# FFN blocks that carry attention: the value products of two tiles in one run, fourteen buffers for exponentials

## The chip, the cores and the metric

The kernel runs on one core of a Trainium2 chip. TensorE (PE) multiplies; ScalarE (ACT), VectorE (DVE) and GpSimd (POOL) work on elements; SyncE (SP) issues nearly all DMAs. Each engine takes its own instructions in order and waits for the others at semaphores. The metric is the device time of one execution in microseconds (us), the median over runs; lower is better.

## The reference

One transformer block on 2048 rows of width 576, in fp32: `h = x + attention(layernorm(x))`, `out = h + ffn(layernorm(h))`.

- Attention has 32 query heads of width 18 and one head of keys and values that all of them share. Scores are scaled by 18^-0.5, softmaxed over all 2048 keys (no mask), multiplied with the values, and projected by `wo` (576 x 576).
- The FFN is a bilinear gate without a nonlinearity: `((x @ w_gate) * (x @ w_up)) @ w_down`, inner width 4608.

## The kernel before

The 2048 rows are four blocks of 512. Keys, values and queries come first, together with the attention of block 0. From then on the FFN of block b is run with the attention of later blocks in between, so that ACT's exponentials lie beside TensorE's FFN products. The last FFN (block 3) has no attention beside it and is written another way (`last_block`). The schedule is the program's own order: the text of the functions sets the order of each engine's instructions, and buffers are rings, so an instruction that takes a buffer waits until the last reader of the old content is done.

**One FFN tile** (`ffn`, loop over `f`, 36 per block) makes 128 of the 4608 inner columns for 512 rows. It has 27 steps `j` (9 slices of the width, each as high*high, high*low and low*high of numbers split into two fp32r parts, called hi and lo). A step is two matmuls at once: the gate product `pg` on rows 0 to 63 of the array and the up product `pu` on rows 64 to 127. While attention is left (`on`), `pg` and `pu` come from a ring of three PSUM banks (`ps_r`), which the down product uses too; later they are two halves of one `gu` tile. At the end of a tile ACT copies `pg` out of PSUM (`g`, line 1063), and DVE multiplies it with `pu` into `hf` (line 1067).

**Two tiles make a pair.** After an odd tile (`k` = 1) the two `hf` are turned into operands `A` (tile `room`): sums `S` on DVE (lines 937 to 940), then splits into hi and lo (`left_first`, `left`, `left_sums`; `split` at lines 96 and 97 casts, and DVE subtracts). At the end of the next even tile the down product of that pair runs (`down`): 42 matmuls, each on the full 128 x 128 array, in 14 stages of three. Every stage's result is added to the residual `h`, by DVE straight from PSUM (line 994), or by an ACT copy into one of the `tmp` buffers (line 998) and a POOL add (line 999). For the last pair of a block the product is a plain one (line 958).

**Attention in between** is counted in pairs of heads: `pair` does two score matmuls of 56 rows side by side (line 701) into one of two score tiles in PSUM (`ps_s`, two banks each), and ACT takes the exponentials of the 128 x 1024 scores into a buffer `P` (line 702). Every two pairs complete one key tile `t`, and `flush` then multiplies the exponentials waiting in `pend` with the values: four matmuls per key tile that each use 32 of the array's columns (line 706); on the chip each of them is two passes, so the trace has 4096 of them for 2048 in the program. Before the change a tile with attention has pairs at `j` = 0, 4, ..., 24 and one after step 26, eight in all, and ends with a flush of four key tiles (32 recorded passes, 8 groups of four).

So TensorE works in three shapes: two halves of 64 rows (FFN and scores), the full array (down, projections `yo` at line 832, transposes at line 888), and four strips of 32 columns (values). The order before is: odd tile, values, even tile, values, down product, and again.

**Weights.** `load_w` loads the gate and up weights of a tile (576 KB) into `wr` (two buffers), `split_w` splits them into `ws` (POOL cast, DVE subtraction); it is called at `j` = 3 for the next tile and starts the load for the tile after it. `load_wd` loads the down weights, seven pieces per pair, into ten `wdo` buffers. `weight_sums` makes sums of weights for the last block with POOL during the first two FFNs.

At the end of a block `spread` transposes the next block's normalised rows (`xh`) into `X`.

Of the kernel before, what the change touches and what calls it, by code (L numbers as in the profile page):

```python
# [57 lines left out]
class Block:  # L58
# [744 lines left out]
    def load_wo_0(self):  # L803

        self.wo_0 = self.wp.tile([P, 2, 5, D], F32R, tag="X", bufs=1, name="wo_0")
        rs = [self.wp.tile([P, 2, D], F32, tag="wr", bufs=2, name=f"wo_r{i}") for i in range(2)]
# [9 lines left out]
    def project(self, b, c):  # L816
# [4 lines left out]
        for s in range(NQ):  # L821
            sl = slice(s * P, (s + 1) * P)
            for n in range(2):
# [9 lines left out]
                if b and c == 4 and (s, n) in ((0, 1), (2, 0)):  # L833
                    z = self.tmp[:, self.n_tmp % 5]
                    self.n_tmp += 1
                    self.act.copy(z, y[:, :HD])
# [28 lines left out]
    def normal(self, b):  # L865
# [3 lines left out]
        for s in range(NQ):  # L869
            xh = self.p_tile([P, 640], f"xh2_{b}_{s}") if b else self.wp.tile([P, 640], F32, tag="wdo", bufs=WD_BUFS, name=f"xh2_0_{s}")  # L870
# [34 lines left out]
    def load_w(self, n):  # L905

        if n < NF * (NB - 1):
            r = self.wr[n] = self.wp.tile([P, 9, P], F32, tag="wr", bufs=2, name=f"wr{n}")
            self.sp.dma_start(r, self.wgu[n % NF])

    def split_w(self, n):
        if n < NF * (NB - 1):
# [3 lines left out]
            self.load_w(n + 2)  # L916
# [9 lines left out]
    def left_first(self, n, hf):  # L926

        m = 2 if plain(n) else 1
        self.split(self.A[:, 0, 0:m], self.A[:, 1, 0:m], hf[:, 0:m * HT].rearrange("p (a q) -> p a q", a=m))

    def left(self, n, hf):
# [9 lines left out]
        self.split(A[:, 0, m:m + 2], A[:, 1, m:m + 2], hf[1].rearrange("p (a q) -> p a q", a=2))  # L941

    def left_sums(self):
        self.split(self.A[:, 0, 3:7], self.A[:, 1, 3:7], self.S)

    def down(self, b, pair):
# [4 lines left out]
        if pair == NC - 1:  # L951
# [8 lines left out]
            def add(s, n):  # L960
                hs, y = h[:, s, n * HD:(n + 1) * HD], ys.pop((s, n))[:, :HD]
                if n:
                    z = self.tmp[:, self.n_tmp % 5]
# [20 lines left out]
        for i, (t, bank, (x, w), first, (s, n), on_dve) in enumerate(STAGES):  # L984
# [10 lines left out]
            else:  # L995
                z = self.tmp[:, self.n_tmp % 5]
# [5 lines left out]
    def room(self):  # L1002
# [5 lines left out]
        self.tmp = self.hh.tile([P, 5, HD], F32, tag="tmp", bufs=1, name="tmp")  # L1008
        self.n_tmp = 0

    def ffn(self, b):
# [6 lines left out]
        for f in range(NF):  # L1018
# [12 lines left out]
            for c in range(9):  # L1031
                for wk, xk in ((0, 0), (0, 1), (1, 0)):
                    if on and not last and j % 4 == 0 and self.more(b + 2):
# [15 lines left out]
                    if j == 21 and b == f == 0:  # L1049
                        self.flush(len(self.pend))  # L1050
# [11 lines left out]
            g = self.hh.tile([P, TB], F32, tag="g", bufs=1, name=f"g{n_}")  # L1062
            act.copy(g, pg)  # L1063
# [11 lines left out]
            self.flush(len(self.pend))  # L1075
# [6 lines left out]
        if end:  # L1082
            del X, pg, pu, gu, w, ps, hf, g, self.X
# [8 lines left out]
    def ahead(self):  # L1092
# [58 lines left out]
        for i in range(-LEAD, 0):  # L1151
            if i == 4 - LEAD:
                yield
                sets = [self.wp.tile([P, 4 * HT], F32R, tag="wr", bufs=2, name=f"wrs{i}") for i in range(2)]
# [50 lines left out]
    def down_pairs(self, b, pairs):  # L1205
# [4 lines left out]
        for i, (bank, (x, w), first, (s, n)) in enumerate(QUAD):  # L1210
            W = [self.wdo.pop((b, p, w)) for p in pairs]
            for t in range(2):
# [9 lines left out]
                else:  # L1222
                    z = self.tmp[:, self.n_tmp % 5]
# [8 lines left out]
    def last_block(self, ahead, D):  # L1232
# [45 lines left out]
        for p in range(NC):  # L1278
# [73 lines left out]
            g = self.hh.tile([P, TB], F32, tag="g", bufs=1, name=f"gl{p}")  # L1352
# [125 lines left out]
    def run(self):  # L1478
# [16 lines left out]
        with ExitStack() as st:  # L1495
# [8 lines left out]
            self.G = cp.tile([P, 64], F32R, name="G")  # L1504
            self.mx = cp.tile([H, 8], F32, name="mx")
            st.enter_context(tc.manual_schedule())
            with tc.tile_pool(name="p0q", bufs=1) as self.p0q:
                self.wq_in, self.wq = self.wq, {}
                self.XT = [self.p0q.tile([P, 9, TB], F32R, tag=f"XT{b}", name=f"XT{b}") for b in range(NB)]
                with tc.tile_pool(name="qb", bufs=2) as self.qb:  # L1510
# [24 lines left out]
            self.wp, self.hh, self.p2 = pool("w", 2), pool("hid", 4), pool("P2", 1)  # L1535
# [19 lines left out]
            self.load_w(1)  # L1555
# [12 lines left out]
            self.split_w(0)  # L1568
            self.cast = self.act.copy
# [14 lines left out]
P_BUFS = 6  # L1584

# [4 lines left out]
WD_BUFS = 10  # L1590
# [145 lines left out]
```

## Time and profile before

| | before |
|---|---|
| median of 3 runs | 2279.18 us (2277.54 to 2280.16) |
| span of the profiled execution | 2277.7 us |
| TensorE matmul busy | 2251.0 us, 99% of the span |
| ACT / DVE / POOL busy | 66% / 56% / 32% |
| exponentials (line 702) | 1024, 1027 ns each |
| value passes (line 706) | 4096 |
| down products (line 988) | 2142 matmuls, 51 runs of 42 |

The span runs from the first to the last instruction of the profiled execution; it is the time of that execution that the page gives, 1.5 us under the median of the timed runs. Matmuls are pipelined and their ends are modelled, so "busy" does not say how fast TensorE works: the distance from one start to the next does. PE is the matmul, PEld the loading of its weights. In a row of groups the numbers after the bar are busy time and the mean duration of one instruction in ns, then idle time before them. In a row of the timeline stand the start in us, the duration in us, the engine, the line, and the count of instructions that follow each other; a bracket shows idle time before, and what ended it.

### The profile page before, as it was taken

What the parts mean: (1) busy time and instruction counts of PE and PEld (TensorE: products, weight loads), DVE (VectorE), ACT (ScalarE), POOL (GpSimd) and SP (SyncE); (2) the same over time, 40 slices, a digit from 0 to 9 for tenths busy, and PEclk for the clock granted to TensorE, in tenths of its full rate; (3) what the DMA queues carried; (4) which work ended last, traced back from release to release, by engine and by line L of the source; (5) the groups of instructions that cost most, each with busy time, mean ns of one, the idle gap of its engine ahead of it and who ended that gap; (6) DMA issues with size and microseconds to landing.
All of it is one profiled execution on the core that took longest, in us unless ns stands there. A gap on an engine that the chain in (4) does not pass through costs nothing.

```text
span 2277.7 us, 46397 instructions
## 1 busy us (share of the span) xinstructions
PE 2251.0 (99%) x17972; PEld 1640.2 (72%) x17972; DVE 1267.0 (56%) x2184; ACT 1512.4 (66%) x2061; POOL 719.5 (32%) x820
## 2 busy tenths in 40 slices
PE   7999999999999999999999999999999999999999
PEld 5333345777677777777777777777777788999999
DVE  8555645444445446454545455544434477778776
ACT  7888876767676766667666766667676724555553
POOL 4445401333233333323333332322222244222222
PEclk9999999999999999999999999999999999999999
DMA  5879843545455554645555544654343345677775
GB/s 175 266 247 300 287 162 99 168 157 158 158 172 166 164 180 149 206 140 168 165 164 171 167 160 146 204 175 145 113 126 109 105 160 174 207 247 237 233 248 172
DMA packets 200438, 407.05 MB, mean 179 GB/s; under 512 B 22638, under 2 KB 54510, under 8 KB 200214
## 3 DMA queue, kind: packets, MB, share of 16 engines
q1 hardware_dynamic: 197621, 393.42, 54.0%
q0 software_dynamic: 2592, 10.62, 1.5%
q8 instruction: 143, 2.34, 0.4%
q14 instruction: 82, 0.66, 0.1%
HBM read 317.27 MB, written 74.55 MB: 172 GB/s over the span
## 4 chain that ended last, share of the span: by engine, by line
PE 83%; DVE 2%; ACT 1%; issue 0%; DMA 0%; SPq 0%; POOL 0%; ACTq 0%; DVEq 0%
PE pg L1036 23%; PE acc L706 15%; PE y L988 13%; PE s L701 9%; PE gs L1252 8%; PE yq L1217 4%; PE pu L1036 3%; PE yo L832 3%; PE gu L1036 2%; PE gs L1259 2%; PE y L958 1%; ACT P L702 1%; PE tx L888 0%; DVE room L97 0%; DVE ws L97 0%
## 5 line engine op out<-in xcount | busy, mean ns | idle before, releaser
L702 ACT ACTIVATE P<-s 128x1024 f32<-128x1024 f32 x1024 | 1025.6, 1027 | 273.7 <-PE s L701 195.3
L1036 PE MATMUL pu<-X,ws 64*128 64x512 f32 x2565 | 694.3, 390 | 0.0
L1036 PE MATMUL pg<-X,ws 64*128 64x512 f32 x2565 | 693.5, 389 | 0.1
L1036 PEld LDWEIGHTS pg<-X,ws 64*128 64x128 f32 x2565 | 476.2, 186 | 72.5 <-DMA wsum<-in_wgs_dram 0.8
L706 PE MATMUL acc<-P,V 128*32 128x512 f32 x4096 | 491.0, 599 | 0.7 <-ACT P L702 0.6
L1036 PEld LDWEIGHTS pu<-X,ws 64*128 64x128 f32 x2565 | 473.8, 186 | 4.9 <-ACT tmp L965 0.3
L701 PE MATMUL s<-q,kT 56*128 56x512 f32 x2048 | 441.5, 422 | 4.6 <-ACT P L702 3.5
L999 POOL TENSOR_TENSOR h<-h,tmp 128x288 f32<-128x288 f32 x306 | 238.4, 807 | 598.2 <-ACT tmp L998 597.1
L701 PEld LDWEIGHTS s<-q,kT 56*128 56x128 f32 x2048 | 199.7, 184 | 203.3 <-ACT P L702 118.8
L988 PEld LDWEIGHTS y<-wdo,room 128*128 128x128 f32 x2142 | 289.6, 188 | 43.2 <-issue 34.8
L988 PE MATMUL y<-wdo,room 128*128 128x288 f32 x2142 | 303.6, 300 | 1.3 <-DVE h L994 1.3
L706 PEld LDWEIGHTS acc<-P,V 128*32 128x32 f32 x4096 | 114.8, 109 | 246.9 <-issue 234.4
L994 DVE TENSOR_TENSOR h<-h,y 128x288 f32<-128x288 f32 x408 | 176.1, 453 | 199.8 <-PE y L988 199.6
L998 ACT COPY tmp<-y 128x288 f32<-128x288 f32 x306 | 122.1, 399 | 240.8 <-PE y L988 222.3
L1067 DVE TENSOR_TENSOR hf<-pu,g 128x512 f32<-128x512 f32 x95 | 65.7, 692 | 303.1 <-ACT g L1063 303.1
L96 POOL CAST ws<-wr 128x1152 fp32r<-128x1152 f32 x108 | 127.1, 1177 | 315.0 <-PE pu L1036 238.2
L97 DVE TENSOR_TENSOR ws<-wr,ws 128x1152 fp32r<-128x1152 f32 x108 | 184.6, 1709 | 64.0 <-POOL ws L96 59.7
L1200 POOL TENSOR_TENSOR wsum<-wsum,wsum 128x512 f32<-128x512 f32 x72 | 99.7, 1385 | 137.6 <-DMA wsum<-in_wgs_dram 137.4
L97 DVE TENSOR_TENSOR room<-S,room 128x1024 fp32r<-128x1024 f32 x51 | 62.5, 1226 | 132.8 <-ACT room L96 132.8
L1217 PE MATMUL yq<-wdo,XW 128*128 128x288 f32 x504 | 86.1, 297 | 0.1
L1036 PE MATMUL gu<-X,ws 64*128 64x512 f32 x702 | 82.0, 390 | 0.0
L839 DVE TENSOR_TENSOR h<-h,yo 128x288 f32<-128x288 f32 x154 | 63.4, 452 | 30.1 <-PE yo L832 26.8
(262 smaller groups left out, 2633.3 us busy)
## 6 DMA issues: line engine op xcount, KB each, us to landing
wdo<-wd_dram SPq DMA_DIRECT2D x492, 288.0 KB
wr<-in_wgu_dram SPq DMA_DIRECT2D x108, 576.0 KB
wsum<-in_wgs_dram SPq DMA_DIRECT2D x108, 256.0 KB
wd_dram<-wd_room SPq DMA_DIRECT2D x20, 1008.0 KB
wsum_dram<-wsum SPq DMA_DIRECT2D x72, 256.0 KB
raw<-wsum_dram SPq DMA_DIRECT2D x72, 256.0 KB
q<-q_dram SPq DMA_DIRECT2D x64, 216.0 KB
raw<-in_wgs_dram SPq DMA_DIRECT2D x54, 256.0 KB
```

The source lines that it names most:

```text
L96: (copy or self.cast)(hi, src)
L97: self.dve.tensor_tensor(lo, src, f32(hi), ALU.subtract)
L701: self.pe.matmul(s_[:, i], self.kT[o:o + 56, t * P:(t + 1) * P], q[o:o + 56, pr], start=True, stop=True)
L702: self.act.activation(p_, s_, AF.Exp, scale=SCALE)
L706: self.pe.matmul(acc[32 * j:32 * j + 32, :], self.V[:, t, :], Ps[j // 2][:, j % 2, :], start=(t == 0), stop=(t == NT - 1), skip_group_chec ...
L988: pe.matmul(y[:, :HD], m[:, t * P:(t + 1) * P], k, start=(first and j == 0), stop=(j == 2), skip_group_check=True)
L994: dve.tensor_tensor(hs, hs, y[:, :HD], ALU.add)
L998: act.copy(z, y[:, :HD])
L999: pool.tensor_tensor(hs, hs, z, ALU.add)
L1036: pe.matmul(ps, w[o:o + 64, wk, c], X[o:o + 64, xk, c], start=(j == 0), stop=(j == 26))
L1217: pe.matmul(y[:, :HD], A[:, k, x, t * P:(t + 1) * P], v[:, l], start=(first and z == j == 0), stop=(z == len(pairs) - 1 and j == 2), skip_ ...
L1252: pe.matmul(bank[:, g * HT:(g + 1) * HT], W[:, wk, c, g], X[:, 2 * xk + c], start=(first and g == c == wk == xk == 0), stop=(c == 1 and wk ...
```

## The change

- In a tile with attention, an odd tile no longer flushes (`if not k or last`). The value products of two tiles (eight key tiles) run together at the end of the even tile, in front of the down product.
- The pairs stand at other steps: in an even tile at `j` = 0, 4, ..., 20 and two after step 26, in an odd tile as before (0, 4, ..., 24 and one after step 26). The last tile of a block, which had none, gets eight pairs at every third step, and a flush.
- The ring of buffers for exponentials grows from 7 to 14 (`P2_BUFS` = 8 beside the 6 of `P_BUFS`).
- Room for it: one `wr` buffer instead of two (the load of tile n + 2 is now issued at `j` = 14, or 9 without attention, after the split of tile n + 1); nine `wdo` instead of ten; three `tmp` instead of five; no `g`, ACT copies `pg` into `hf`, and DVE multiplies in place; `G` in a pool that is given back; 2048 bytes of scratch for DMA descriptors per partition.
- The casts of `left_first`, `left` and `left_sums` move from ACT to POOL (line 96).

TensorE at the end of an odd tile. Here `s` are scores, `pg` and `pu` the FFN products, `acc` the values; the first three rows are steps of the odd tile, the last ones of the even tile that follows. Before:

```order
L1036 MATMUL pg_15526<-X_10340,ws_15333 128x512
L1036 MATMUL pu_15527<-X_10340,ws_15333 128x512
L701 MATMUL s_0_3_1_15649<-q_0_14923,kT 128x512 x2
L706 MATMUL acc_0_15662<-P_0_0_0_15529,V 32x512 x2
L706 MATMUL acc_0_15662<-P_0_0_1_15547,V 32x512 x2
L706 MATMUL acc_0_15662<-P_0_1_0_15562,V 32x512 x2
L706 MATMUL acc_0_15662<-P_0_1_1_15576,V 32x512 x2
L706 MATMUL acc_0_15662<-P_0_2_0_15604,V 32x512 x2
L706 MATMUL acc_0_15662<-P_0_2_1_15618,V 32x512 x2
L706 MATMUL acc_0_15662<-P_0_3_0_15636,V 32x512 x2
L706 MATMUL acc_0_15662<-P_0_3_1_15650,V 32x512 x2
L701 MATMUL s_0_4_0_15683<-q_0_14923,kT 128x512 x2
```

and in the change:

```order
L1035 MATMUL pg_15493<-X_10336,ws_15285 128x512
L1035 MATMUL pu_15494<-X_10336,ws_15285 128x512
L701 MATMUL s_0_3_1_15616<-q_0_14894,kT 128x512 x2
L701 MATMUL s_0_4_0_15632<-q_0_14894,kT 128x512 x2
L1035 MATMUL pg_15630<-X_10336,ws_15508 128x512
L1035 MATMUL pu_15631<-X_10336,ws_15508 128x512
```

The values are gone from this place; the last scores of the odd tile, the first scores of the even tile and its first `pg` and `pu` follow each other. Over the whole program the array's shape changes 567 times before and 471 times in the change. The joined run of two tiles stands in the program 44 times.

ACT at the same place, before:

```order
L702 ACTIVATE P_0_3_0_15636<-s_0_3_0_15635 128x1024
L1063 COPY g_15647<-pg_15526 128x512
L702 ACTIVATE P_0_3_1_15650<-s_0_3_1_15649 128x1024
L96 CAST room<-hf_15654 128x512
L96 CAST room<-ob_10593 128x512
L702 ACTIVATE P_0_4_0_15684<-s_0_4_0_15683 128x1024
L702 ACTIVATE P_0_4_1_15702<-s_0_4_1_15701 128x1024
L702 ACTIVATE P_0_5_0_15715<-s_0_5_0_15714 128x1024
L96 CAST room<-S 128x1024
L702 ACTIVATE P_0_5_1_15731<-s_0_5_1_15730 128x1024
```

and in the change:

```order
L702 ACTIVATE P_0_3_0_15603<-s_0_3_0_15602 128x1024
L1062 COPY hf_15614<-pg_15493 128x512
L702 ACTIVATE P_0_3_1_15617<-s_0_3_1_15616 128x1024
L96 CAST room<-ob_10586 128x512
L702 ACTIVATE P_0_4_0_15633<-s_0_4_0_15632 128x1024
L702 ACTIVATE P_0_4_1_15649<-s_0_4_1_15648 128x1024
L702 ACTIVATE P_0_5_0_15662<-s_0_5_0_15661 128x1024
L702 ACTIVATE P_0_5_1_15678<-s_0_5_1_15677 128x1024
```

The casts of `hf` and `S` have left ACT's queue; the order of exponentials and of the copy of `pg` among each other is the same.

POOL in FFN tiles without attention (block 2, near its end), one row after another. Before, its queue holds the casts of two tiles' weights and the six adds of a down product, here for two pairs:

```order
L96 CAST ws_26397<-wr_26007 128x1152
L96 CAST ws_26526<-wr_26155 128x1152
L999 TENSOR_TENSOR h_16896<-h_16896,tmp 128x288 x6
L96 CAST ws_26730<-wr_26400 128x1152
L96 CAST ws_26868<-wr_26529 128x1152
L999 TENSOR_TENSOR h_16896<-h_16896,tmp 128x288 x6
```

and in the change, for one pair:

```order
L96 CAST ws_28344<-wr_28217 128x1152
L96 CAST room<-hf_28332 128x256
L96 CAST room<-hf_28406 128x512
L96 CAST room<-S 128x1024
L96 CAST ws_28426<-wr_28363 128x1152
L998 TENSOR_TENSOR h_16912<-h_16912,tmp 128x288 x6
```

Three casts of the operands now stand in front of the second weight cast and of the adds.

The diff, cut to its core:

```diff
-        i = self.p_next = (self.p_next + 1) % (P_BUFS + (self.p2 is not None))
+        i = self.p_next = (self.p_next + 1) % (P_BUFS + (P2_BUFS if self.p2 is not None else 0))
...
     def load_w(self, n):
...
-            r = self.wr[n] = self.wp.tile([P, 9, P], F32, tag="wr", bufs=2, name=f"wr{n}")
+            r = self.wr[n] = self.wp.tile([P, 9, P], F32, tag="wr", bufs=1, name=f"wr{n}")
...
             self.split(w[:, 0], w[:, 1], r, self.nc.gpsimd.tensor_copy)
-            self.load_w(n + 2)
...
     def left_first(self, n, hf):
...
-        self.split(self.A[:, 0, 0:m], ..., a=m))
+        self.split(self.A[:, 0, 0:m], ..., a=m), self.nc.gpsimd.tensor_copy)
...
     def left_sums(self):
-        self.split(self.A[:, 0, 3:7], self.A[:, 1, 3:7], self.S)
+        self.split(self.A[:, 0, 3:7], self.A[:, 1, 3:7], self.S, self.nc.gpsimd.tensor_copy)
...
-                    z = self.tmp[:, self.n_tmp % 5]
+                    z = self.tmp[:, self.n_tmp % NTMP]
...
     def ffn(self, b):
...
-                    if on and not last and j % 4 == 0 and self.more(b + 2):
+                    if on and j in (PAIRS[2] if last else PAIRS[k]) and self.more(b + 2):
                         self.pair()
...
                     if j == 3:
                         self.split_w(n_ + 1)
+                    if j == (14 if on else 9):
+                        self.load_w(n_ + 2)
...
-                    if j == 21 and b == f == 0:
-                        self.flush(len(self.pend))
...
-            g = self.hh.tile([P, TB], F32, tag="g", bufs=1, name=f"g{n_}")
-            act.copy(g, pg)
-            if on and not last and self.more(b + 2):
-                self.pair()
             hf = self.hh.tile([P, TB], F32, tag="hf", bufs=2, name=f"hf{n_}")
-            dve.tensor_tensor(hf, pu, g, ALU.mult)
+            act.copy(hf, pg)
+            if on and not last:
+                for _ in range(1 if k else 2):
+                    if self.more(b + 2):
+                        self.pair()
+            dve.tensor_tensor(hf, pu, hf, ALU.mult)
...
-            self.flush(len(self.pend))
+            if not k or last:
+                self.flush(len(self.pend))
...
+P2_BUFS = 8
-WD_BUFS = 10
+WD_BUFS = 9
+NTMP = 3
+PAIRS = (range(0, 24, 4), range(0, 28, 4), range(0, 24, 3))
...
-    nc = _bacc.Bacc("TRN2", target_bir_lowering=False, num_devices=1)
+    nc = _bacc.Bacc("TRN2", target_bir_lowering=False, num_devices=1, dynamic_dma_scratch_size=2048)
```

More of the change, by code (lines that the diff above doesn't have):

```diff
@@ L805, in load_wo_0 @@
         self.wo_0 = self.wp.tile([P, 2, 5, D], F32R, tag="X", bufs=1, name="wo_0")
[L806 removed]
+        rs = [self.wp.tile([P, 2, D], F32, tag=("wr", "ws")[i], bufs=1 + i, name=f"wo_r{i}") for i in range(2)]
         rs.append(self.wp.tile([P, 1, D], F32, tag="wor", bufs=1, name="wo_r2"))
@@ L869, in normal @@
         for s in range(NQ):
-            xh = self.p_tile([P, 640], f"xh2_{b}_{s}") if b else self.wp.tile([P, 640], F32, tag="wdo", bufs=WD_BUFS, name=f"xh2_0_{s}")
+            xh = self.p_tile([P, 640], f"xh2_{b}_{s}")
             self.dve.tensor_scalar(xh[:, 0:D], h[:, s, :], mv[:, s, 0:1], rs[:, s:s + 1], ALU.subtract, ALU.mult)
@@ L1153, in ahead @@
                 yield
-                sets = [self.wp.tile([P, 4 * HT], F32R, tag="wr", bufs=2, name=f"wrs{i}") for i in range(2)]
+                sets = [self.wp.tile([P, 4 * HT], F32R, tag="wr", bufs=1, name="wrs0"), self.p2.tile([P, 4 * HT], F32R, tag="P2", name="wrs1")]
                 sets += [self.o_hl.rearrange("p k q -> p (k q)")]
```

22 lines of the change are left out of this document (11 added, 11 removed).

## The prediction

> **What bounds the kernel now.** I read the page first, then who waited in the stretch with FFN and attention (400 to 1830 us), then the timeline of one boundary.
>
> ```profile
> PE 2251.0 (99%) x17972; PEld 1640.2 (72%) x17972; DVE 1267.0 (56%) x2184; ACT 1512.4 (66%) x2061; POOL 719.5 (32%) x820
> PE 83%; DVE 2%; ACT 1%; issue 0%; DMA 0%; SPq 0%; POOL 0%; ACTq 0%; DVEq 0%
> 400.00:1830.00 1430.00, 1428.02 (x11780) 1041.99 (x11778) 689.85 (x1154) 976.67 (x1262) 440.25 (x469) 1.00 0.50 158
> PE yo L832 <- ACT tmp L836: 0.6, 2, 0.3
> ```
>
> TensorE sets the end: 99% busy, 83% of the chain of waits. In the stretch it is busy 1428.0 of 1430.0 us, and its longest sum of waits is 0.6 us. Clock 1.00, so no gain is hidden there. What can move is how many starts lie how far apart. A whole boundary, odd tile to even tile, on TensorE:
>
> ```profile
> 818.37 0.42 PE L701 MATMUL s<-q,kT 56*128 56x512 f32 x2
> 818.60 0.39 PE L1036 MATMUL pg<-X,ws 64*128 64x512 f32 x1
> 818.83 0.39 PE L1036 MATMUL pg<-X,ws 64*128 64x512 f32 x1
> 819.06 0.39 PE L1036 MATMUL pg<-X,ws 64*128 64x512 f32 x1
> 819.29 0.42 PE L701 MATMUL s<-q,kT 56*128 56x512 f32 x2
> 819.64 3.64 PE L706 MATMUL acc<-P,V 128*32 128x512 f32 x32
> 820.52 1.90 PE L706 MATMUL acc<-P,V 128*32 128x512 f32 x16
> 821.38 1.47 PE L706 MATMUL acc<-P,V 128*32 128x512 f32 x12
> 823.21 0.50 PE L701 MATMUL s<-q,kT 56*128 56x512 f32 x2
> 823.55 0.39 PE L1036 MATMUL pg<-X,ws 64*128 64x512 f32 x1
> 823.78 0.39 PE L1036 MATMUL pg<-X,ws 64*128 64x512 f32 x1
> ```
>
> The 820.52 and 821.38 rows are the same run of values entered later: its third and fifth group of four. So a group of values takes (821.38 - 820.52) / 2 = 0.43 us; a step of FFN or scores 0.23 us (818.60 to 818.83).
>
> **The change, part by part.**
>
> *Fewer changes of shape.* From the last scores of the odd tile (819.29) to the second step of the even one (823.78) are 4.49 us. Without a change of shape the same work is 8 x 0.43 + 3 x 0.23 = 4.13. So one excursion into values costs 0.36 us: 0.12 before the first group, 0.02 in it, 0.11 after the last, 0.11 after the first scores. The joined run removes it 44 times: **-15.8 us**. The values themselves stay. Of the 96 changes of shape that go, 88 are these; the other eight, at half of 0.36 each, give **-1.4**. At two block ends the tile that had no attention now has a run of values between its last step and the transposes, where TensorE now waits for ACT's copy:
>
> ```profile
> 912.54 0.39 PE L1036 MATMUL pu<-X,ws 64*128 64x512 f32 x1
> 913.48 0.41 PE L888 MATMUL tx<-C,xh 128*128 128x128 f32 x2 [0.55 <-ACT g L1063]
> ```
>
> That is 2 x 0.55: **-1.1**. The eight pairs themselves are taken from later tiles and cost the same there.
>
> *What the values covered.* At the joined boundary the scores of the even tile are the third within 1.15 us, and there are two score tiles in PSUM. ACT at the same boundary:
>
> ```profile
> 818.83 1.03 ACT L702 ACTIVATE P<-s 128x1024 f32<-128x1024 f32 x1
> 819.75 0.58 ACT L1063 COPY g<-pg 128x512 f32<-128x512 f32 x1
> ```
>
> Call the scores at 818.37 T. Their exponentials start at T + 0.46 and end at T + 1.49; the copy of `pg` follows at T + 1.38 and ends at T + 1.96 (the two overlap by 0.1). In the change both keep their places in ACT's queue. Two rules of release come from two other places:
>
> ```profile
> 705.38 1.04 ACT L96 CAST room<-S 128x1024 fp32r<-128x1024 f32 x1
> 706.32 1.03 ACT L702 ACTIVATE P<-s 128x1024 f32<-128x1024 f32 x1
> 707.17 0.39 PE L1036 MATMUL pg<-X,ws 64*128 64x512 f32 x1
> 707.40 0.50 PE L701 MATMUL s<-q,kT 56*128 56x512 f32 x2
> 707.73 0.40 PE L1036 MATMUL pg<-X,ws 64*128 64x512 f32 x1
> 922.71 0.39 PE L1036 MATMUL pg<-X,ws 64*128 64x512 f32 x1
> 922.99 0.50 PE L1036 MATMUL pu<-X,ws 64*128 64x512 f32 x1
> 923.00 0.73 PE L1036 MATMUL pg<-X,ws 64*128 64x512 f32 x2
> 923.33 0.39 PE L1036 MATMUL pu<-X,ws 64*128 64x512 f32 x1
> ```
>
> Scores start 0.05 after the exponentials two before them end (706.32 + 1.03 to 707.40), and a step behind scores that have just waited comes 0.33 later, not 0.23. At 922.71 a `pu` comes 0.28 behind its `pg`: the next `pg` goes along with it, and the next `pu` comes 0.34 behind.
>
> Now the boundary in the change. The odd tile's last scores stand at T + 0.92. The even tile's would stand at T + 1.15; they wait for T's exponentials, until T + 1.54. `pg` follows at T + 1.87. Its `pu` takes the bank of the odd tile's `pg` (three banks in turn: odd `pg`, odd `pu`, even `pg`, then again), so it waits for the copy: T + 2.01. The next `pu` then comes at T + 2.35. Unhindered it would be at T + 0.92 + 3 x 0.23 = T + 1.61. Loss **0.74 us** a boundary. Queued behind the waiting scores is all of TensorE; who waits for it is nobody but the end. It isn't made up later: the exponentials of the odd tile's last scores end at T + 2.89 (1.86 + 1.03), those of the even tile's first at T + 3.8, and the scores that need their tiles come at T + 3.04 (2.35 + 3 x 0.23) and T + 4.2, so TensorE goes on at its own pace, 0.74 late. Bounds: nothing, if something I don't see lets ACT run ahead; 0.49 (0.39 for the scores and 0.10 for the step behind them) if the copy costs nothing. I take 0.74, since every duration has a row: 44 x 0.74 = **+32.6**.
>
> The Trainium skill ("TensorE: Matmul & The Clock Gate", Part 3, The mechanism) has it that TensorE's reorder window pulls weight loads ahead of matmuls in flight. By that the steps behind the two waits would lose no 0.10, the boundary would cost 0.64 at most, and the end would come 4.4 us earlier; the 0.33 at 707.40 speaks against it.
>
> *Casts leave ACT.* The wait at 707.40 stands behind the cast of `S` at 705.38, once per pair of tiles: 0.10 us that go, 44 x 0.10 = **-4.4**. Everything else ACT gains is off the path.
>
> *The same casts on POOL, and one `wr`.* POOL takes 1.15 us for a weight cast where ACT takes 1.04 for `S`, and is 32% busy. With attention the operands have the even tile, 16 groups of values (6.9 us) and wait for nobody; the one weight buffer leaves some 5 us from `j` = 14 to the next `j` = 3 (21 steps of 0.23), against 5.3 us for a load of that size in the last row below, and a late split has the rest of the even tile, the values and the down product behind it: 0, and a lateness of more than those 15 us would count if they were gone. Without attention nothing lies between. Before, in such a pair:
>
> ```profile
> 1916.77 1.23 DVE L97 TENSOR_TENSOR room<-S,room 128x1024 fp32r<-128x1024 f32 x1 [0.52 <-ACT room L96]
> 1917.91 1.35 DVE L97 TENSOR_TENSOR ws<-wr,ws 128x1152 fp32r<-128x1152 f32 x1
> 1919.78 0.81 DVE L994 TENSOR_TENSOR h<-h,y 128x288 f32<-128x288 f32 x2
> 1920.28 0.54 PE L988 MATMUL y<-wdo,room 128*128 128x288 f32 x2 [0.23 <-DVE h L994]
> L96 POOL CAST ws<-wr x94: 1136/1147/1622, 417.5 to 1828.0; 128x1152 fp32r<-128x1152 f32 x94
> L937 DVE TENSOR_TENSOR S<-hf,hf x45: 424/426/1337, 426.5 to 1829.3; 128x256 f32<-128x256 f32 x45
> wd_room<-in_wd_dram POOLq DMA_DIRECT2D x10, 576.0 KB, 5.3
> ```
>
> The down product already waits 0.23 for DVE's first add, which stands behind the `S` and weight subtractions. In the change POOL casts `S`, then at once the weights; an `S` operation on DVE that takes 426 ns in the middle takes up to 1337 (the sixth row), so the engines do hold each other up. If POOL's weight cast goes first, DVE's subtraction is 1.15 late, and so is TensorE. From nothing (cast and subtraction slip past each other) to 2.3 (both subtractions late, one cast each). I take one cast, 1.15, between the ends: 7 down products without attention, **+8.0**.
>
> *Three `tmp`, nine `wdo`, less scratch.* Two down products, and the adds:
>
> ```profile
> 683.82 5.96 PE L988 MATMUL y<-wdo,room 128*128 128x288 f32 x42
> 713.48 5.91 PE L988 MATMUL y<-wdo,room 128*128 128x288 f32 x42
> L999 POOL TENSOR_TENSOR h<-h,tmp x36: 800/807/824, 626.7 to 781.8; 128x288 f32<-128x288 f32 x36
> ```
>
> Fourteen stages in 5.9 us are 0.42 each, and six of them copy, so one copy comes per 0.98 us against adds of 0.81: three buffers suffice, two pieces of down weights are still ahead, and the scratch serves 18 early loads on a POOL that is mostly idle: 0. If POOL is late there, ACT's copy is late by as much as the term before already counts.
>
> Sum: -15.8 - 1.4 - 1.1 + 32.6 - 4.4 + 8.0 = +17.9, against the profiled span of 2277.7, which lies 1.5 under the median of 2279.2. Forecast **2297 us**, slower by 0.8%.
>
> **The rivals.**
>
> *The boundary costs nothing, and the change does what it seems to.* One mechanism: ACT, rid of its casts, has T's exponentials and the copy ready before the even tile begins. For it: ACT is 66% busy. Against: T's exponentials start 0.46 behind T's scores already now, with no queue ahead of them. It decides from a boundary under 0.36. Then -15.8 - 1.4 - 1.1 - 4.4 = -22.7: **2256 us**, or 2264 with the POOL term. On the other side of no change.
>
> *The boundary costs just the scores* (0.49): -22.7 + 21.6 = -1.1, **2278 us** without the POOL term. For it: the copy ends just 0.14 behind the `pg` it could delay.
>
> *DVE and POOL shut each other out.* Both subtractions late: 7 x 2.3 = 16.1, the sum +26: **2305 us**. For it the 1337; against it, that the middle value shows no hold.
> The Trainium skill ("SBUF — State Buffer", Who interferes with whom) says that a DVE instruction with two SBUF inputs and a GpSimd one that reads SBUF exclude each other for whole instructions, whoever starts first. `S` and both subtractions are of that kind; the trace agrees, 426 against 1337 ns, and it speaks against moving these casts to POOL.
>
> **How the numbers follow.** Forecast 0.42; boundary free 0.24; just the scores 0.18; shut out 0.16. About 0.2% (4.6 us) is what a measurement tells from no change. Faster by more: nearly all of the free boundary, and a little of the scores' case, 0.25. Within: most of the scores' case and the low edge of the forecast, 0.17. Slower: the rest, 0.58. The slow cases alone reach from 2285 to 2312 (the POOL term at nothing, at 2.3, and some delay more); the range is drawn down to 2261, so that a part of the free boundary with the POOL term is in.
>
> **What would show it.** The distance from the odd tile's last scores to the even tile's second step: 1.43 us with the scores waiting for ACT if I am right, 0.69 if the boundary is free. Runs of 64 value passes in front of the down products, and down products 30.0 us apart where they now are 29.66 (683.82 to 713.48). In the tiles without attention a wait of the down product for DVE of about a microsecond. It would be wrong if ACT's exponentials at the boundary started less than 0.46 behind their scores, or if `pu` didn't wait for the copy.

## The result and the profile after

The changed kernel takes **2314.21 us** (median; 2313.73 to 2314.79), the kernel before 2279.14 us beside it: a ratio of 1.0155, with a 95% interval of 1.0141 to 1.0170, so slower by 35.1 us. The forecast was 2297 us, slower by 18, with a range up to 2312. The sign was right; the size was half of what came. The profiled execution spans 2311.9 us, so its trace carries the loss.

The page of the changed kernel: its engines, and the first line of the chain that ended last.

```profile
PE 2258.3 (98%) x17972; PEld 1660.3 (72%) x17972; DVE 1347.6 (58%) x2184; ACT 1418.9 (61%) x1902; POOL 897.6 (39%) x979
PE 77%; DVE 3%; ACT 3%; POOL 2%; issue 2%; DMA 1%; SPq 0%; ACTq 0%; POOLq 0%; DVEq 0%
```

ACT has lost 94 us of work and POOL gained 178, as the casts moved. DVE has the same 2184 instructions and is 81 us longer busy with them: something holds it. TensorE's share of the chain is down from 83% to 77%, so the end now hangs on other engines in places. Which, the waits of TensorE tell (us in all, times, longest); first the stretch with attention, from 400 to 1830 us:

```profile
PE s L701 <- ACT P L702: 14.8, 47, 4.4
```

then what follows, from 1820 to 2010 us:

```profile
PE y L987 <- DVE h L993: 11.4, 6, 3.0
PE y L987 <- ACT tmp L997: 2.1, 1, 2.1
```

In the first row stand 46 short waits of scores for exponentials and a single long one of 4.4. In the second view the down products wait for DVE's adds, 11.4 us in six of them, and once for a `tmp`. Where in time the loss arises is read by holding the same instruction of both traces side by side:

| place | changed kernel behind the one before, us |
|---|---|
| first FFN step | -1.0 |
| first down product | -2.7 |
| 17th, near the end of the first FFN | +5.3 |
| 18th, in the second FFN | +16.6 |
| 34th | +21.1 |
| 45th, the first without attention | +17.1 |
| first product of the last block | +35.0 |
| end | +34.2 |

Eight pairs and their values now stand earlier, in the last tile of two blocks (some 5 us each, 4.8 at the first), and 11.2 us come back between the 44th and the 45th product (+28.3 to +17.1); they nearly cancel. So there are three losses: a slow drift with attention, a step of about 6.5 us between the 17th and the 18th product (16.6 - 5.3 - 4.8), and 17.9 us in the tiles without attention.

**The drift: one joined boundary.** TensorE in the changed kernel, the same pairs as in the prediction's first timeline, and ACT beside it:

```profile
821.43 0.41 PE L701 MATMUL s<-q,kT 56*128 56x512 f32 x2
822.36 0.41 PE L701 MATMUL s<-q,kT 56*128 56x512 f32 x2
822.95 0.50 PE L701 MATMUL s<-q,kT 56*128 56x512 f32 x2 [0.19 <-ACT P L702]
823.29 0.39 PE L1035 MATMUL pg<-X,ws 64*128 64x512 f32 x1
823.43 0.50 PE L1035 MATMUL pu<-X,ws 64*128 64x512 f32 x1
823.77 0.39 PE L1035 MATMUL pu<-X,ws 64*128 64x512 f32 x1
```

```profile
822.80 0.58 ACT L1062 COPY hf<-pg 128x512 f32<-128x512 f32 x1
```

With T = 821.43 the third scores start at T + 1.52 (forecast 1.54), `pg` at T + 1.86 (1.87), `pu` at T + 2.00 (2.01), just behind the copy that ends at T + 1.95, the next `pu` at T + 2.34 (2.35). Note that the wait is printed as 0.19 and the loss is 0.73: the list of waits counts idle time only, and a late step that keeps the array busy with longer rows isn't in it. And between two down products:

```profile
655.50 5.93 PE L987 MATMUL y<-wdo,room 128*128 128x288 f32 x42
678.38 7.08 PE L706 MATMUL acc<-P,V 128*32 128x512 f32 x64
685.38 5.95 PE L987 MATMUL y<-wdo,room 128*128 128x288 f32 x42
```

The values stand in one run of 64, and the products are 29.9 us apart, where the same two were 29.6 apart before. The next two, those of the prediction's 29.66, are 30.2 apart (30.0 forecast).

**The step at the start of the second FFN.** TensorE, then ACT, in the changed kernel:

```profile
955.69 0.39 PE L1035 MATMUL pg<-X,ws 64*128 64x512 f32 x1
960.50 0.80 PE L701 MATMUL s<-q,kT 56*128 56x512 f32 x2 [4.42 <-ACT P L702]
961.10 0.62 PE L1035 MATMUL pg<-X,ws 64*128 64x512 f32 x1
```

```profile
958.91 0.62 ACT L96 CAST room<-ob 128x512 fp32r<-128x512 f32 x1 [4.30 <-DMA ob<-ob]
959.43 2.99 ACT L702 ACTIVATE P<-s 128x1024 f32<-128x1024 f32 x3
```

At the end of an odd tile ACT is given the cast of a finished chunk of heads. The DMA that puts the chunk together has not landed, ACT works in order, and three exponentials queue behind the cast; with both score tiles full, TensorE stands still for 4.42 us. ACT's waits for that DMA in the whole run, in the kernel before, in the change, and in the run below in which every tile has its own values:

```profile
ACT room L96 <- DMA ob<-ob: 0.2, 1, 0.2
ACT room L96 <- DMA ob<-ob: 7.0, 4, 4.3
ACT room L96 <- DMA ob<-ob: 6.5, 4, 4.0
```

So the long wait was not there before: this cast started at 963.79, 6.7 us behind the issue of the last of its five DMAs. In the change ACT reaches it at 954.61, when the first of the five is just being issued (954.63). The wait is there with or without joined tiles. Joining leaves TensorE with all of it: with values in every tile TensorE waits only 1.1 us at this place. That the eight pairs in the last tile of the block brought the cast forward is likely from the order of the program; it was not run alone.

The matmuls behind the gap are slow, 0.62 where they take 0.39. The stretch as a window (us; busy time and count of PE, PEld, DVE, ACT, POOL; granted clock; DMA share; GB/s):

```profile
960.50:965.50 5.00, 5.00 (x30) 4.08 (x32) 1.53 (x1) 3.51 (x4) 2.14 (x2) 0.68 0.90 266
```

The clock is at 0.50 for some three of these five microseconds, 0.68 in the mean: 5.0 x 0.32 = 1.6 us more. 4.42 + 1.6 is most of the step.

**The tiles without attention.** DVE's subtractions by form there (min/median/max in ns), in the changed kernel:

```profile
L97 DVE TENSOR_TENSOR room<-S,room x7: 2134/2135/2160, 1831.9 to 1969.8; 128x1024 fp32r<-128x1024 f32 x7
```

and the kernel before:

```profile
L97 DVE TENSOR_TENSOR room<-S,room x6: 1212/1225/1227, 1832.5 to 1935.6; 128x1024 fp32r<-128x1024 f32 x6
```

The subtraction of `S` takes 2135 ns where it took 1225, every time and nearly to the same nanosecond. That isn't noise but a lock. One of them, on POOL and DVE in the changed kernel:

```profile
1903.06 1.44 POOL L96 CAST room<-S 128x1024 fp32r<-128x1024 f32 x1 [1.01 <-DVE S L939]
1904.45 1.14 POOL L96 CAST ws<-wr 128x1152 fp32r<-128x1152 f32 x1
```

```profile
1902.92 0.68 DVE L97 TENSOR_TENSOR room<-hf,room 128x512 fp32r<-128x512 f32 x1
1904.54 2.13 DVE L97 TENSOR_TENSOR room<-S,room 128x1024 fp32r<-128x1024 f32 x1 [0.94 <-POOL room L96]
1906.60 1.35 DVE L97 TENSOR_TENSOR ws<-wr,ws 128x1152 fp32r<-128x1152 f32 x1
1907.86 0.81 DVE L993 TENSOR_TENSOR h<-h,y 128x288 f32<-128x288 f32 x2
```

POOL's weight cast begins the moment the cast of `S` ends, 0.09 ahead of the subtraction that waited for the same event. It ends at 1905.59, and from there the subtraction takes 1.08 us: it stood until the cast was through. The weight subtraction (1.35, as long as before) and the first add follow. The hold works the other way as well: POOL's cast of `S` took 1.44, as it began 0.14 behind DVE's subtraction of `hf`; where no subtraction stands in front (at 963.88, say) it takes 1.04. TensorE at this product, the 48th:

```profile
1905.82 1.45 PE L987 MATMUL y<-wdo,room 128*128 128x288 f32 x9
1908.36 2.68 PE L987 MATMUL y<-wdo,room 128*128 128x288 f32 x18 [1.09 <-DVE h L993]
1913.12 2.28 PE L987 MATMUL y<-wdo,room 128*128 128x288 f32 x15 [2.09 <-ACT tmp L997]
```

The first gap, 1.09 us, is the plain case; three of the seven products have it. The second is a `tmp` that POOL has not yet emptied: between its weight cast and its adds POOL runs sixteen small operations of the last block's layernorm here (lines 117 to 127, from 1905.69 to 1911.85).

### The profile page after: what moved, and what is told of

Same layout as the page of the kernel before. It is cut to its first block, busy times and chain, and to the rows that moved or that the text cites. A ratio compares the mean times of both kernels' runs of the same rounds, so it can differ in the third digit from the quotient of the medians.

```text
span 2311.9 us, 45915 instructions
## 1 busy us (share of the span) xinstructions
PE 2258.3 (98%) x17972; PEld 1660.3 (72%) x17972; DVE 1347.6 (58%) x2184; ACT 1418.9 (61%) x1902; POOL 897.6 (39%) x979
## 3 DMA queue, kind: packets, MB, share of 16 engines
q8 instruction: 143, 2.34, 0.4%
## 4 chain that ended last, share of the span: by engine, by line
PE 77%; DVE 3%; ACT 3%; POOL 2%; issue 2%; DMA 1%; SPq 0%; ACTq 0%; POOLq 0%; DVEq 0%
PE pg L1035 16%; PE acc L706 15%; PE y L987 12%; PE s L701 8%; PE gs L1253 8%; PE pu L1035 6%; PE yq L1218 4%; PE yo L832 3%; ACT P L702 2%; PE gu L1035 2%; PE gs L1260 1%; DVE ws L97 1%; PE y L957 1%; POOL h L998 1%; POOL room L96 1%
## 5 line engine op out<-in xcount | busy, mean ns | idle before, releaser
L1035 PE MATMUL pu<-X,ws 64*128 64x512 f32 x2511 | 680.0, 392 | 0.0
L1035 PE MATMUL pg<-X,ws 64*128 64x512 f32 x2511 | 674.7, 389 | 0.1
L1035 PEld LDWEIGHTS pg<-X,ws 64*128 64x128 f32 x2511 | 462.7, 186 | 46.1 <-ACT tmp L964 0.4
L1035 PEld LDWEIGHTS pu<-X,ws 64*128 64x128 f32 x2511 | 460.2, 186 | 25.0 <-ACT hf L1062 7.9
L987 PE MATMUL y<-wdo,room 128*128 128x288 f32 x2142 | 309.6, 303 | 14.4 <-DVE h L993 11.4
L96 POOL CAST room<-hf 128x256 fp32r<-128x256 f32 (+1 forms) x108 | 68.4, 633 | 336.8 <-DVE hf L1067 336.8
L1067 DVE TENSOR_TENSOR hf<-pu,hf 128x512 f32<-128x512 f32 x93 | 63.8, 686 | 198.5 <-ACT hf L1062 198.5
L1201 POOL TENSOR_TENSOR wsum<-wsum,wsum 128x512 f32<-128x512 f32 x72 | 146.5, 2034 | 47.9 <-DMA wsum<-in_wgs_dram 38.9
L717 DVE STREAM_TRANSPOSE os<-acc 128x512 f32<-128x512 f32 x32 | 22.9, 717 | 149.5 <-PE acc L706 149.5
L1035 PE MATMUL gu<-X,ws 64*128 64x512 f32 x810 | 94.5, 389 | 0.0
L97 DVE TENSOR_TENSOR room<-hf,room 128x256 fp32r<-128x256 f32 (+1 forms) x108 | 90.7, 840 | 2.9 <-POOL room L96 2.9
```

The source lines that it names most:

```text
L96: (copy or self.cast)(hi, src)
L97: self.dve.tensor_tensor(lo, src, f32(hi), ALU.subtract)
L987: pe.matmul(y[:, :HD], m[:, t * P:(t + 1) * P], k, start=(first and j == 0), stop=(j == 2), skip_group_check=True)
L1035: pe.matmul(ps, w[o:o + 64, wk, c], X[o:o + 64, xk, c], start=(j == 0), stop=(j == 26))
L1201: pool.tensor_tensor(to, x, y, op)
```

## The experiments

**Casts back on ACT where there is no attention.**

```diff
             on = self.more(b + 2)
+            self.caster = self.nc.gpsimd.tensor_copy if on else act.copy
...
-        self.split(self.A[:, 0, 3:7], self.A[:, 1, 3:7], self.S, self.nc.gpsimd.tensor_copy)
+        self.split(self.A[:, 0, 3:7], self.A[:, 1, 3:7], self.S, self.caster)
```

(The two casts of `hf` alike.)

> The change, but in the tiles without attention the casts of hf and S stand on ACT again (with attention they stay on POOL). If POOL's casts are what delays the seven down products without attention, the 17.9 us that the change lost between down product 44 and the last block come back: 2296 us (2306 if they are worth only the 8.0 of the prediction). If the single weight buffer or the three tmp delay them, nothing comes back: 2314.

2299.64 us: 14.6 come back. The same view of DVE in this run:

```profile
L97 DVE TENSOR_TENSOR room<-S,room x7: 1218/1226/1228, 1832.3 to 1955.1; 128x1024 fp32r<-128x1024 f32 x7
```

1226 ns again. Between the 45th product and the last block this trace loses 1.75 us against the kernel before (17.66 to 19.41 behind), where the change lost 17.9. With the casts on ACT nearly all of the loss there is gone, though the three `tmp` and the single `wr` are still in this run. By the times it is 14.6 us, nearly twice the 8.0 of the prediction.

**Every tile runs its own values again.**

```diff
-            if not k or last:
-                self.flush(len(self.pend))
+            self.flush(len(self.pend))
```

> The change, but every tile runs its own values again, so that no odd-to-even boundary is joined; pairs, casts and buffers stay as in the change. By the prediction a joined boundary loses 0.74 us and saves 0.36: 44 x 0.38 = 16.7 come back, 2297 us; 2291 if the stall of some 6.5 us at the start of the second FFN also hangs on the missing values there. If the boundary is free and the steady stretch is slower for another reason, the 15.8 us of the shape changes are lost again: 2330.

2289.14 us: 25.1 come back, near the 23.2 of the joined boundary together with the step (16.7 + 6.5). The rival, by which joining is a gain, falls by 41 us.

**The chunk of heads half a tile later.**

```diff
-(LANDING if b == 0 and c < 4 else 0)
+(LANDING if b == 0 and c < 4 else min(b, 1))
```

> The change, but a finished chunk of heads (from the second block on) is cast on ACT one round, half a tile, later. If the stall at the start of the second FFN comes from ACT, which waits 4.3 us at a joined boundary for the DMA of that chunk with the exponentials behind it, 4.3 to 6.5 us come back: 2308 to 2310 us. If that stall has another cause, it stays: 2314.

2305.55 us: 8.7 come back, more than the step alone. TensorE's waits from 400 to 1800 us in this run:

```profile
PE s L701 <- ACT P L702: 8.9, 44, 0.3
```

The long wait is gone; 44 short ones are left, all but one of them at a joined boundary. Against the kernel before, this trace is 6.2 us slower over the first FFN's sixteen periods (from -2.7 to +3.5) and the one with its own values in every tile 0.3 faster (-3.1 to -3.4): 6.5 / 16 = 0.41 a boundary, forecast 0.38. The chunk's cast costs elsewhere too, but less: 8.0 us of drift in the change over the same periods, 6.2 here.

**The weight split behind the sixth stage of the down product.**

```diff
-                    if j == 3:
+                    if j == 3 and (on or not todo):
                         self.split_w(n_ + 1)
...
-                drain(self.down(b, *todo))
+                for i, _ in enumerate(self.down(b, *todo)):
+                    if i == 5:
+                        self.split_w(n_ + 1)
```

> The change, but in the tiles without attention that have a down product the weight split is issued behind the sixth stage of the down product instead of behind step 3; all casts stay on POOL. If POOL's weight cast and DVE's subtraction of S hold each other up, that subtraction goes from 2.13 us back to 1.23, the weight subtraction of 1.35 no longer stands before the first add, and 7 x 2.25 = 15.8 us come back: 2298 us. If the delay is POOL's slower cast of S alone (1.44 for 1.05, some 0.4 later), the subtraction stays at 2.13 and only the 1.35 in front of the adds is gained: 2305.

2337.76 us, 23.5 slower than the change, where both theories had it faster. DVE by form without attention, and TensorE's waits from 1800 to 2010 us:

```profile
L97 DVE TENSOR_TENSOR room<-S,room x7: 1224/1226/1682, 1833.0 to 1991.4; 128x1024 fp32r<-128x1024 f32 x7
```

```profile
PE y L987 <- DVE h L993: 26.1, 8, 3.8
```

The hold is gone (1226 ns at the median), as the lock has it. But now DVE, in order, waits for POOL's weight cast in the middle of the adds, and POOL's cast stands behind its own adds; TensorE idles over 3.5 us in seven products and starts again at half the clock (0.50 from 1924.50 to 1927.00, behind one of them). The expectation had counted what the split left and not what it was put in front of.

**POOL's casts alone, in the kernel before.**

```diff
-        self.split(self.A[:, 0, 3:7], self.A[:, 1, 3:7], self.S)
+        self.split(self.A[:, 0, 3:7], self.A[:, 1, 3:7], self.S, self.nc.gpsimd.tensor_copy)
```

(The two casts of `hf` alike.)

> The kernel before, with one part of the change alone: the casts of hf and S on POOL in all tiles. Two wr and five tmp buffers stay, each tile runs its own values. If POOL's casts alone delay the down products without attention by the 14.6 us that came back when they went to ACT, and save 0.10 a pair of tiles with attention (4.4), this gives 2279.1 - 4.4 + 14.6 = 2289 us; by the prediction's 8.0 it is 2283. If the single wr or the three tmp are needed for the delay, it is 2275.

2287.02 us, a ratio of 1.0037 (1.0023 to 1.0050). Its trace is 4.3 us ahead of the kernel before when attention ends, and 7.5 behind at the end: -4.3 and +11.8. The first is the 0.10 a pair of tiles of the prediction; it comes evenly, from one down product to the next.

**The same with three `tmp`.**

```diff
-            z = self.tmp[:, self.n_tmp % 5]
+            z = self.tmp[:, self.n_tmp % 3]
```

> The kernel before, with the casts of hf and S on POOL in all tiles and with three tmp buffers in place of five; two wr stay. The prediction has three tmp at nothing: 2287 us, as with POOL's casts alone. If three tmp are part of the price (a wait of 2.1 us for a tmp stands in the trace of the change), 2 to 4 us more: 2289 to 2291.

2291.22 us: 4.2 more. TensorE's waits from 1800 to 1985 us with three:

```profile
PE y L988 <- ACT tmp L998: 2.1, 1, 2.1
```

With five this line is absent, and the other waits are alike (10.4 us for DVE's adds, 10.5 with five). Against the nothing of the prediction stands this wait of 2.1 us. The rest isn't clearly the `tmp`'s: this trace has three falls of the clock, behind gaps of 2.96, 2.82 and 2.39 us, and that of the run with five has one, though its gaps there are as long (2.96, 2.83, 2.39). At 1.7 us each, two falls are 3.4 us, and the last section shows that chance has a hand in them. So three `tmp` cost between 2.1 and 4.2 us. With the upper figure, 11.8 + 4.2 = 16.0 is close to the 16.1 that the change loses there over the run with ACT's casts (17.9 - 1.75), and nothing is left for the single `wr`; with the lower 2.2 us are left, less than the two falls. That is by subtraction; the single `wr` was not tried alone.

**The weight split ahead of the cast of `S`.**

```diff
-                    if j == 3:
+                    if j == (3 if on else 0):
                         self.split_w(n_ + 1)
```

> The change, but in the tiles without attention the weight split is issued in front of step 0, ahead of the cast of S, where it stood behind step 3, after it. All casts stay on POOL. If the price comes from where POOL's weight cast falls (under DVE's subtraction of S, 2.13 for 1.23, with the weight subtraction behind it and in front of the adds), the first add comes 1.3 us earlier in each down product and 9 to 12 us come back: 2302 to 2305 us. If the two engines hold each other up wherever the cast falls, or S on POOL is simply late, nothing comes back: 2314.

2310.64 us: 3.6 back, a third of the 9 to 12 of a better place. DVE by form without attention, this run:

```profile
L97 DVE TENSOR_TENSOR ws<-wr,ws x14: 1352/1668/2189, 1824.2 to 1966.3; 128x1152 fp32r<-128x1152 f32 x14
L97 DVE TENSOR_TENSOR room<-S,room x7: 1210/1212/1680, 1836.5 to 1968.4; 128x1024 fp32r<-128x1024 f32 x7
L938 DVE TENSOR_TENSOR S<-hf x7: 415/1360/1361, 1831.1 to 1964.1; 128x256 f32<-128x256 f32 x7
```

The subtraction of `S` is at 1212 ns. But an `S` operation of 413 ns now takes 1360, under POOL's weight cast, and the weight subtraction up to 2189, under POOL's cast of `S`. The hold does not go; it moves to whatever DVE instruction meets a cast. This is the mechanism of the rival "DVE and POOL shut each other out".

**Two changes of the boundary.** Odd tiles with their last scores two steps earlier:

```diff
-PAIRS = (range(0, 24, 4), range(0, 28, 4), range(0, 24, 3))
+PAIRS = (range(0, 24, 4), (0, 4, 8, 12, 15, 18, 22), range(0, 24, 3))
```

> The change, with the scores of odd tiles in front of steps 0, 4, 8, 12, 15, 18 and 22 where they stood at 0, 4, 8, 12, 16, 20 and 24. Worked by the prediction's rules: the third scores then find their tile free, ACT's copy of pg starts 0.46 behind the last step and not behind the exponentials, and the boundary loses 0.52 in place of 0.74 us: 44 x 0.22 = 9.7 us less, 2304.5 us. If the wait for the score tile were all of the loss, it would be gone: 17 us less or better, 2297.

2304.94 us, against 2304.5. The boundary on TensorE:

```profile
819.13 0.67 PE L701 MATMUL s<-q,kT 56*128 56x512 f32 x4
819.63 0.39 PE L1035 MATMUL pg<-X,ws 64*128 64x512 f32 x1
819.96 0.49 PE L1035 MATMUL pu<-X,ws 64*128 64x512 f32 x1
820.30 0.39 PE L1035 MATMUL pu<-X,ws 64*128 64x512 f32 x1
```

The even tile's scores follow at once (`x4`), and `pu` still waits, 0.33 behind its `pg`. And even tiles with their first scores two steps later:

```diff
-PAIRS = (range(0, 24, 4), range(0, 28, 4), range(0, 24, 3))
+PAIRS = ((2, 6, 10, 14, 17, 20), range(0, 28, 4), range(0, 24, 3))
```

> The change, with the scores of even tiles in front of steps 2, 6, 10, 14, 17 and 20 where they stood at 0, 4, 8, 12, 16 and 20. No third scores stand at the joined boundary any more. By the prediction pu still waits for ACT's copy of the odd tile's pg, the second step still starts at T + 2.35, and the scores that covered 0.23 of it are still to do: 44 x 0.23 = 10.1 us more, 2324 us. If the wait for the score tile is what the boundary costs, 0.39 or more a boundary comes back: 2297 us.

2321.98 us: 7.8 slower than the change, against 10.1, and not 17 faster. TensorE's waits in the whole run, and one boundary:

```profile
PE pu L1035 <- ACT hf L1062: 21.0, 44, 0.6
```

```profile
823.51 0.39 PE L701 MATMUL s<-q,kT 56*128 56x512 f32 x2
825.50 0.50 PE L1035 MATMUL pu<-X,ws 64*128 64x512 f32 x1 [0.45 <-ACT hf L1062]
825.85 0.39 PE L1035 MATMUL pu<-X,ws 64*128 64x512 f32 x1
```

Without third scores in the way the wait for the bank shows itself: 44 times, one a boundary. `pu` at T + 1.99, the next at T + 2.34. Both waits of the prediction are there, and taking one away leaves the other.

**Both repairs together**, the first and the second edit of this section:

> The change, with both repairs: every tile runs its own values, and in tiles without attention the casts are on ACT. If the two effects are separate, 25.1 and 14.6 us come off 2314.2: 2274.5 us, 0.2% under the kernel before. If they overlap (the down products without attention wait for something the joined runs push there), it is 2280 or more.

2273.59 us, a ratio of 0.9978 (0.9967 to 0.9988): faster than the kernel before, by 5.0 us, and 0.9 from the sum. The effects are separate. The chunk's cast still costs here: TensorE waits 1.83 us behind it, with a fall of the clock.

**One part of the change in the kernel before: POOL's casts with attention only.** (The edit of `caster` in the kernel before.)

> The kernel before, with one thing of the change: the casts of hf and S on POOL, in tiles with attention only. With POOL's casts in all tiles, TensorE stood 4.3 us ahead of the kernel before when attention ended, and lost 11.8 behind it. If the gain is the 0.10 per pair of tiles of the prediction, it stays and nothing is lost: 2278.6 - 4.3 = 2274.3 us. If it came from the end of attention being nearer and is given back there, 2278.6.

2274.72 us, a ratio of 0.9983 (0.9974 to 0.9992), 4.0 us less than before. At the prediction's place a step now comes 0.23 behind the scores (705.75 to 705.98), where it was 0.33 (707.40 to 707.73): the wait behind the cast of `S` is gone. A line of choice and three arguments give 4.0 of the 5.0 us that both repairs of the whole change give, and the two intervals overlap.

## Why the prediction was right in sign and wrong in size

Two steps of the sum failed. The casts on POOL without attention were priced at 8.0 us and three `tmp` at nothing; together they measured 14.6. And ACT's queue at the joined boundary was taken to hold nothing that waits for a DMA; a chunk's cast there cost 8.7. That is 15.3 of the 17.2 us by which the sum was short.

*Fewer changes of shape, -15.8, and the boundary, +32.6: right.* Net 16.8 was forecast. Values in every tile gave 25.1 back and the chunk moved gave 8.7, so by subtraction 16.4 belong to the boundary (18 by the 0.41 of the drift). Each of its marks stands within 0.02 us of where it was put, and the runs with moved scores came out within 0.4 and 2.3 us of the same rules. The rivals "boundary free" and "just the scores" fall.

*The casts of `S` that leave ACT, -4.4: right.* -4.3 in one trace, -4.0 in the time of the run with that part alone, and the wait is gone at its place.

*The casts on POOL without attention, +8.0: the mechanism right, the term too small.* It measured 14.6. One cast of 1.15 a product was a fair price for the plain case, whose gap is 1.09. But I multiplied it by seven as if the products were alike. Two of the seven also have the attention's output weights in the queues of POOL and DVE (the subtraction of `wos` takes 1340 ns for 750) and idle 2.96 and 2.82 us; the 48th has 1.09 and 2.09; the 49th, with transposes in front of it, has no gap; the 50th has an operation of the last block in front of the adds and idles 2.35. All gaps sum to 13.5 (11.4 + 2.1 in the waits), where the kernel before has

```profile
PE y L988 <- DVE h L994: 1.3, 3, 0.6
```

And what I had no term for: behind three of the gaps the clock falls. The rows in the changed kernel:

```profile
1837.50:1842.50 5.00, 5.00 (x26) 5.00 (x27) 1.60 (x4) 1.59 (x4) 2.61 (x4) 0.66 0.66 216
1864.10:1869.10 5.00, 4.96 (x25) 4.96 (x26) 1.59 (x4) 1.59 (x4) 2.56 (x4) 0.66 0.67 219
1952.50:1957.50 5.00, 4.99 (x26) 4.99 (x27) 1.67 (x4) 1.59 (x4) 2.94 (x4) 0.66 0.77 253
```

Three times 5.0 x 0.34 are 5.1 us. 13.5 - 1.3 + 5.1 = 17.3, of the 17.9 that the traces differ by there. The case I called "shut out" and put at 0.16 had the mechanism: DVE and POOL exclude each other. That its 16.1 is near the measured size is luck. It had both subtractions late by a cast, 2.3 in each of seven products; in a plain product the trace has one of them held, by 0.91, and it gets the rest from `wos`, the `tmp` and the clock. I had quoted an operation of 426 ns that takes 1337 and then leaned on its median, which tells of the places where no cast met it.

*Three `tmp` for nothing: wrong, 2.1 to 4.2 of the above.* The one copy per 0.98 us against adds of 0.81 leaves three buffers no reserve for a POOL that comes late. In the 48th product the layernorm's operations stand in front of the adds, and the casts put them later still; with the casts on ACT and the same three `tmp` the longest such wait is 0.3. I said that such a delay was already counted in the term before; it was not.

*Missed: the chunk's cast on ACT, 8.7.* My step on what the values covered asked what waits at the boundary for the two tiles and the banks, and took ACT's queue there to be exponentials and a copy. It also holds, once in a few tiles, the cast of a chunk, which waits for a DMA. In the kernel before that cast hardly ever waited (0.2 us in all). The change brought the wait in and took away the values that would have hidden most of it from TensorE; I had looked for neither. I should have listed every kind of instruction that can stand in ACT's queue at that place, and where the change moves it, and not those of the one boundary I had looked at.

*The eight other changes of shape and the block ends, -2.5:* 16.4 - 4.0 + 14.6 + 8.7 = 35.7 against 35.1 measured leaves -0.6 for them. The trace is 2.7 us ahead at the first down product, 1.0 of it before the first FFN step, which no term of mine explains. Part of that is scatter: the kernel before with POOL's casts, which does not differ up to there, is 0.2 behind at that step, and 0.5 ahead with the casts on POOL with attention only. Where the rest goes wasn't followed further.

## What to carry to other kernels

Before a filler is taken out of a queue, list everything that it covers, or would cover once the rest of the change has moved things, on each engine, the rare items and their DMAs too; here the frequent loss was forecast to half a microsecond in all and the rare one was missed. Work moved from an engine to another is worth its price stage by stage: the same casts gained 4 us where POOL was free and DVE far from the path, and lost 14.6 where DVE's subtractions stood in front of TensorE's banks; a choice by stage kept the gain. And a price per occurrence holds for the occurrences that were looked at: look at each when there are seven.

## What the runs showed of the hardware

Two things. **DVE and POOL exclude each other for whole instructions**, not by sharing. A DVE subtraction with two operands in SBUF takes 1.23 us alone and 2.13 under a POOL cast, the cast's remaining 1.05 and then 1.08; moved elsewhere, the same cast makes an operation of 413 ns take 1360. And a POOL cast of 1.04 takes 1.44 when such a subtraction began 0.14 before it. The Trainium skill ("SBUF — State Buffer", Who interferes with whom) states this exclusion, and the trace agrees with it in the instances shown here.

**What a TensorE gap costs in clock hangs on where it falls, and not on its length alone.** By the clock records of the changed kernel the granted clock falls to 0.50 at 960.34, 1837.56, 1864.87 and 1953.62 us, for 3.41 us each time, which loses 1.7. From one fall to the next are 257, 8 and 26 steps of 3.413 us. The change and ten of the experiments have such falls behind the first 300 us, 34 in all; where a trace has several they lie on a grid of this step, which stands elsewhere in every run, and the clock stays low for one step or two. A fall comes at the end of a step in which TensorE idled for just over half of it: in front of each of the 34 stands a step with 1.82 us of idle time or more, and no step at full clock with 1.77 or less is followed by one. So a gap of 2.96 us (to 1834.40) cost nothing in the run with POOL's casts alone, as it was split between two steps, with 1.33 and 1.69 us idle; and one of 1.83 us brought a fall in the run with both repairs. The second of the two steps, then the step of the shorter gap and the one behind it:

```profile
1832.71:1836.12 3.41, 1.72 (x13) 1.72 (x13) 2.45 (x5) 0.57 (x2) 0.68 (x2) 1.00 0.69 225
949.62:953.03 3.41, 1.58 (x14) 1.02 (x12) 0.69 (x1) 2.59 (x4) 0.00 (x0) 1.00 0.60 157
953.03:956.45 3.42, 3.42 (x18) 2.68 (x18) 1.02 (x1) 1.85 (x3) 2.13 (x2) 0.50 0.86 261
```

The Trainium skill ("TensorE: Matmul & The Clock Gate", Part 1, What's actually happening) puts the fall behind at least one idle window of some 3.4 us; the step here has that length, but a little over half of it idle was enough, and the measurement decides. The idle times rest on the modelled ends of matmuls.
